# Two-layer decode kernel: stationary operands of up to 32 columns, gate and up as rows, and a new written-out order

## The chip, the cores and the metric

The kernel runs on one core of a Trainium2 chip, in one launch. The metric is device time in microseconds (us), the median over executions; lower is better. The profile and its trace are of one execution on that core. Engines are named as in the profile: PE (matrix products), DVE, ACT and POOL (vector work), SP (which issues the transfers); SPq is SP's queue.

## The reference, cut to what matters

Two layers with the same weights and the same K and V caches are run one after the other on 4 tokens (B = 4, one position each, D = 448):

```python
x = x + _A_ref(_layernorm(x), k_cache, v_cache, wq, wo)     # 16 query heads, 8 kv heads of 256
x = x + _B_ref(_layernorm(x), w_gate, w_up, w_down)         # (silu(x @ w_gate) * (x @ w_up)) @ w_down, F = 1792
x = x + _A_ref(_layernorm(x), k_cache, v_cache, wq, wo)
x = x + _B_ref(_layernorm(x), w_gate, w_up, w_down)
```

Attention looks only at the last 2048 of 8192 cached positions: `q = x @ wq`, scores `q k / 16`, softmax, times v, then `@ wo`. So each token has, for each of 8 kv heads, 1 MB of K and 1 MB of V; both layers read the same ones. All data are bf16.

## The kernel before, in words

**Storage and loads.** K and V come in halves of 512 KB: two K halves and two V halves for each token and kv head. A pool of 31 slots holds such halves; 7 further slots of the same size first hold `wq`. Of a token's 8 heads the K and V of 6 stay in their slots from layer 0 to layer 1 (`KEEP_K`, `KEEP_V`), so 160 half loads are made and not 256. All transfers go through SP's one queue, in the order of `SEQ_SP` (L121), and `SLOTS` (L130) gives the slot of each. `schedule` (L235) makes a load wait for the last PE operation that reads what its slot held before (`rel`): scores for a K half, a PV operation for a V half. SP works in order, so a load that waits holds back every load behind it.

**The unit of work: a group of two kv heads** (`group`, L929), written `t l k`, so `010+011` is token 0, layer 1, heads 0 and 1. DVE transposes each K half in place (L948). POOL spreads the query over the columns of `qe` (L987). PE makes the scores S (L982): 32 products of 128 rows by 8 columns with 256 moving columns, four quadrants of the array side by side. DVE takes the maximum, PE spreads it (L1000, L1003), DVE negates it, ACT makes the exponentials (L1013), PE turns them (L1026), ACT copies them to `pT` (L1035), PE and DVE sum them, PE multiplies with V in four operations PV00, PV01, PV10, PV11 (L1057; 32 products in all, each operation for one V half). ACT and DVE pick the wanted rows (L1072, L1074), PE turns ("flip", L1080), DVE scales into a buffer `oT` (L1090). The out-projection of one kv head is either four products with `oT` as stationary operand ("oprow", L1110) or 16 products with `wo` as stationary operand ("opcol", L1102). There are two buffers `oT`; each kv head of a step takes the next in turn, and out-projections come at the end of the step.

**A boundary.** When the last group of a token's layer is done, the rows gathered in bank A are turned ("rowT", L857 to L871), added to the residual (L877), normed (L579 on), sent through the feed-forward part (`ffn`, L767) and normed again; the query projection (`qproj`, L643; 32 products of 512 moving columns, L671) gives the query of layer 1 by two turns (L687) and a spread ("qspread", L701), and a cast to `qc` (L706). Only then can the scores of that token's layer 1 run, and so free the slots of the six heads that were kept. Gate and up (L785) each take 56 products with a 128x128 block of weights as stationary operand and 32 moving columns; tanh is made by ACT (L805), and down (L826) takes 56 products. With `late` (before: token 3 only, and the last layer) gate and up start from the raw residual, and a product `wm` corrects the mean afterwards; `QLATE` does the same for the query projection.

**The order.** `PLAN` lists steps of groups. What each engine does, and in which order, is written out by number in `SEQ_PE`, `SEQ_DVE`, `SEQ_ACT`, `SEQ_POOL` and `SEQ_SP` (L61 to L129); the durations in the code serve only to place the waits. A `w` in `SEQ_PE` is a filler (L1212 on, rows L1214): a product of 512 moving columns with a zero operand, accumulated into bank A, which keeps PE busy while it would wait. `HELD` (L136) says which operations on bank A stand behind which filler.

**Sequence of the tokens.** Token 0's layer 0, token 1's first heads, then the boundary of token 0; its layer 1 together with token 1's layer 0, and so on. While a token passes its boundary, PE works on one group of the next token, and SP loads ahead as far as slots are free. `wd`, the down weights, is the last weight to be loaded.

## Time and profile before

| | |
|---|---|
| median of 3 executions | 284.23 us (284.0 to 289.03) |
| the profiled execution: span | 283.0 us, some 1.2 us less than the median |
| mean granted PE clock | 0.895 |
| moved on SP's queue | 96.06 MB, busy for 88.0% of the span |
| PE busy | 210.4 us (74%) |
| DVE busy | 168.6 us (60%), of it 98.0 us in 80 transposes of K halves |
| ACT, POOL busy | 50.9 us, 77.2 us |
| fillers on PE (L1214) | 147, 51.0 us |
| scores (L982), PV (L1057) on PE | 40.8 us and 42.2 us, 1040 and 1024 products |

How to read it: the span runs from the first to the last instruction of one execution. Busy times of engines overlap. A busy PE is not a PE at its peak, since products are pipelined and their ends are modelled; four products that run side by side in the four quadrants count once. The granted clock is 1.00 at full speed and about half of that in cold stretches. In a window row come its bounds, its length, the busy time of each engine with the number of its instructions, the granted clock, the share of time that the 16 DMA engines were busy, and GB/s. In a row of an engine's timeline come start and length in us, engine, line, operation, output and inputs, shape and count; in square brackets stands the idle time before it and what ended it. Rows of waits give total, times and the longest. "xN" counts instructions.

### The profile page before, as it was taken

Reading aid. Unit: us, or ns where it says so; the run is one execution under the profiler, and the core shown is the slowest. Engines: PE = TensorE matmul, PEld = TensorE weight load, DVE = VectorE, ACT = ScalarE, POOL = GpSimd, SP = SyncE. Lnnn points to the kernel's source line nnn. Section 1 sums busy time; section 2 is a strip of 40 time slices with the busy share of each in tenths; the row PEclk is TensorE's granted clock in tenths of the full one; section 3 lists DMA queues with packets and bytes.
Section 4 is the critical chain, followed back from the end, with each engine's and each line's share of the span. In section 5 each row is a group of like instructions: output and inputs, shape, how many; then the busy total and the mean of one; then the engine's idle time right before and its main releaser. Section 6 shows DMA issues by size and latency. Waiting matters only on the chain.

```text
span 283.0 us, 9526 instructions
## 1 busy us (share of the span) xinstructions
PE 210.4 (74%) x4204; PEld 120.8 (43%) x4204; DVE 168.6 (60%) x511; ACT 50.9 (18%) x123; POOL 77.2 (27%) x202
## 2 busy tenths in 40 slices
PE   0757557586778886789887876798685787888986
PEld 0322124233644543347453432375453346554672
DVE  8745374158226795573755858656756378548831
ACT  0030002011102412112121212112130221034311
POOL 1352103001303432013253241123341221341650
PEclk9997757779789999799997979999795999999995
DMA  6999999999999999968799999948799997899300
GB/s 258 424 414 401 413 410 402 407 401 406 377 390 408 400 408 406 409 278 307 290 324 403 411 406 408 397 170 295 254 316 412 415 405 266 286 341 415 125 2 3
DMA packets 27752, 96.67 MB, mean 342 GB/s; under 512 B 2747, under 2 KB 6847, under 8 KB 26431
## 3 DMA queue, kind: packets, MB, share of 16 engines
q1 hardware_dynamic: 27703, 96.06, 88.0%
q8 instruction: 33, 0.54, 0.8%
q14 instruction: 8, 0.07, 0.1%
q10 hardware_dynamic: 8, 0.00, 0.0%
HBM read 96.05 MB, written 0.00 MB: 339 GB/s over the span
## 4 chain that ended last, share of the span: by engine, by line
DMA 30%; PE 27%; SPq 23%; DVE 12%; issue 3%; ACT 3%; POOL 0%
DMA half<-in_A_k_cache_dram 13%; DMA half<-in_A_v_cache_dram 11%; SPq L555 10%; DVE half L948 8%; SPq L958 8%; DMA wd_sb<-in_B_w_down_dram 6%; PE A L1214 5%; PE Y L1057 5%; PE S L982 4%; PE Z L785 3%; SPq L944 3%; SPq L942 3%; PE Z L826 2%; PE A L1110 2%; DVE oh L1074 1%
## 5 line engine op out<-in xcount | busy, mean ns | idle before, releaser
L948 DVE STREAM_TRANSPOSE half<-half 128x1024 uint32<-128x1024 uint32 x80 | 98.0, 1233 | 16.3 <-DMA half<-in_A_k_cache_dram 15.9
L1214 PE MATMUL A<-identb,small 128*128 128x512 bf16 x147 | 51.0, 452 | 7.4 <-DVE A L478 5.5
L1070 POOL TENSOR_TENSOR small<-small 128x4 f32<-128x4 f32 x32 | 32.4, 1015 | 68.0 <-DVE small L1048 61.7
L982 PE MATMUL S<-half,qe 128*8 128x256 bf16 (+1 forms) x1040 | 40.8, 305 | 12.0 <-DVE half L948 11.1
L1057 PE MATMUL Y<-half,pT 128*8 128x256 bf16 x1024 | 42.2, 296 | 7.3 <-DMA half<-in_A_v_cache_dram 3.9
L982 PEld LDWEIGHTS S<-half,qe 128*8 128x8 bf16 x1040 | 25.4, 92 | 26.1 <-DVE half L948 15.5
L987 POOL TENSOR_TENSOR qe<-qc,tiny 128x64 bf16<-128x64 bf16 x64 | 17.2, 292 | 60.1 <-PE S L982 46.4
L1013 ACT ACTIVATE praw<-S,small 104x256 bf16<-104x256 f32 x32 | 15.1, 473 | 81.7 <-DVE small L1009 81.2
L1057 PEld LDWEIGHTS Y<-half,pT 128*8 128x8 bf16 x1024 | 22.2, 90 | 17.8 <-DMA half<-in_A_v_cache_dram 5.3
L995 DVE TENSOR_REDUCE tiny<-S 104x1 bf16<-104x256 f32 x32 | 13.3, 418 | 19.0 <-PE S L982 19.0
L1072 ACT ACTIVATE oh<-Y 128x256 bf16<-128x256 f32 x32 | 12.3, 383 | 66.3 <-PE Y L1057 61.9
L1214 PEld LDWEIGHTS A<-identb,small 128*128 128x128 bf16 x147 | 13.0, 109 | 20.4 <-issue 7.4
L1074 DVE SCALAR_TENSOR_TENSOR oh<-oh,small,Y 128x256 bf16<-128x256 bf16 x32 | 15.0, 468 | 11.0 <-ACT oh L1072 10.4
L1110 PE MATMUL A<-wo_sb,oT 128*4 128x448 bf16 x220 | 17.2, 380 | 0.8 <-DVE oT L1090 0.6
L1080 PE MATMUL Y<-tiny,oh 128*128 128x4 bf16 x64 | 6.6, 172 | 15.1 <-DVE oh L1074 15.0
L1048 DVE TENSOR_REDUCE small<-Y 128x4 f32<-128x64 f32 x32 | 7.0, 218 | 13.8 <-PE Y L1043 12.1
L1026 PE MATMUL Y<-selt,praw 104*64 104x48 bf16 x256 | 10.1, 197 | 5.9 <-ACT praw L1013 5.5
L1080 PEld LDWEIGHTS Y<-tiny,oh 128*128 128x128 bf16 x64 | 4.2, 103 | 22.5 <-DVE oh L1074 19.6
L1035 ACT ACTIVATE pT<-Y 128x192 bf16<-128x192 f32 x32 | 10.5, 329 | 15.6 <-PE Y L1026 15.3
L1026 PEld LDWEIGHTS Y<-selt,praw 104*64 104x64 bf16 x256 | 6.7, 113 | 12.6 <-ACT praw L1013 9.9
L671 PE MATMUL Z<-half,xn 128*5 128x512 bf16 x160 | 10.2, 379 | 2.2 <-DVE st L606 0.8
L612 POOL TENSOR_SCALAR st<-st 128x1 f32<-128x1 f32 x16 | 4.4, 274 | 26.4 <-DVE st L606 26.4
(125 smaller groups left out, 219.7 us busy)
## 6 DMA issues: line engine op xcount, KB each, us to landing
half<-in_A_v_cache_dram SPq DMA_DIRECT2D x80, 512.0 KB, 12.1
half<-in_A_k_cache_dram SPq DMA_DIRECT2D x66, 512.0 KB, 10.3
half<-in_A_k_cache_dram SPq DMA_DIRECT2D x7, 1024.0 KB, 17.2
wo_sb<-in_A_wo_dram SPq DMA_DIRECT2D x8, 448.0 KB, 16.8
half<-in_A_wq_dram SPq DMA_DIRECT2D x3, 1024.0 KB, 9.0
wd_sb<-in_B_w_down_dram SPq DMA_DIRECT2D x1, 1568.0 KB, 17.1
wg_sb<-in_B_w_gate_dram SPq DMA_DIRECT2D x1, 1344.0 KB, 17.3
wu_sb<-in_B_w_up_dram SPq DMA_DIRECT2D x1, 1344.0 KB, 16.6
```

The source lines that it names most:

```text
L555: g.dma(rank, nbytes, lambda e: e.dma_start(dst, src), f"w{nw[0]}", w=key if isinstance(key, tuple) else (key,), run=run)
L948: return e.transpose(a, a)
L958: g.dma(pp + VLAG, 1 << 19, lambda e, cell=cell, hv=hv, vsrc=vsrc: e.dma_start(unit(cell), vsrc[hv]), None, w=(f"v{t}_{kvh}_{hv}",), run=4 ...
L982: last = e.matmul(Sb[s_][qd:qd + 8, c0:c0 + rhs.free_size()], lhsT=qe[q_][:, P, ce, :, :].rearrange("p a n -> p (a n)"), rhs=rhs, start=(c ...
L987: g.op(POOL, 0.25, pos - SLEAD - 1, lambda e, P=P, t=t, kvh=kvh: e.tensor_tensor(qe[q_][:, P, :, :, :], qc[t][:, kvh, :, :].unsqueeze(2).b ...
L1013: return e.activation(praw[0:R, 0:128 * n].rearrange("p (g r l) -> p g r l", g=2 * n, l=2), Sb[s_][0:R, 0:128 * n].rearrange("p (l g r) -> ...
L1026: last = e.matmul(Yb[p_][64 * h:64 * h + 64, c0:c0 + (48 if n == 2 else 32)], lhsT=praw[0:R, 64 * gg:64 * gg + 64], rhs=w, start=(gg == 0) ...
L1057: last = e.matmul(Yb[p_][32 * gg:32 * gg + M, 256:512], lhsT=pT[pt][:, gg, 2 * a + hv, 4 * P:4 * P + M] if n == 2 else p1[:, gg % 2, 2 * a ...
L1070: g.op(POOL, 0.69, pos, lambda e: e.tensor_tensor(ri[p_][:, 0:2 * n], rs[p_][:, 0:2 * n], expo[:, 1:1 + 2 * n], op=ALU.pow), r=(f"rs{p_}", ...
L1074: g.op(DVE, 0.43, pos, lambda e: e.scalar_tensor_tensor(out=oh[:, :], in0=oh[:, :], scalar=lomask[:, 0:1], in1=Yb[p_][:, 256:512], op0=ALU ...
L1110: last = e.matmul(Ab[32 * k:32 * k + B, 0:D], lhsT=oT[oi][:, k % 2, k // 2, :], rhs=wo_sb[:, 4 * kvh + k, :], start=False, stop=False, ski ...
L1214: return e.matmul(Ab[:, 0:512], lhsT=zero[:, 0:1].broadcast_to([128, 128]), rhs=identb[:, :].unsqueeze(1).broadcast_to([128, 4, 128]), sta ...
```

## The change

**Columns.** The stationary operands of scores, PV and query projection are read as up to 32 neighbouring columns of their buffer, and no longer as 8 (scores, PV) or 5 (query); the row out-projection reads up to 16, before 4. The further columns give further output rows within the same 32-row quadrant of the bank, which nobody reads. For this the buffers become flat (`qef`, `pTf`, `oTf`, `xnx`).

```diff
+COLS = 32
...
-lhsT = xn[:, cc, :]
...
-last = e.matmul(zb[32 * j:32 * j + B + 1, 0:512], lhsT=lhsT, rhs=wq_sb[:, c:c + 512],
+last = e.matmul(zb[32 * j:32 * j + x_cols(cc, j).shape[1], 0:512], lhsT=x_cols(cc, j), rhs=wq_sb[:, c:c + 512],
...
-last = e.matmul(Yb[p_][32 * gg:32 * gg + M, 256:512],
-                lhsT=pT[pt][:, gg, 2 * a + hv, 4 * P:4 * P + M] if n == 2 else
...
+c0 = 48 * gg + 12 * (2 * a + hv) + 4 * P
+c1 = min(c0 + COLS, 192)
+last = e.matmul(Yb[p_][32 * gg:32 * gg + c1 - c0, 256:512], lhsT=pTf[pt][:, c0:c1],
```

**Gate and up as rows.** The 112 products with weights as stationary operand become 32 products with x as stationary operand and 448 moving columns of weights, in four quadrants. Then come a copy of the gate's bank by ACT, a turn by PE, a copy of up's bank (one half by ACT, one by DVE), a second turn; the products `wm` of the late mean stand behind the turns. The down weights are laid out to match, and come in 6 transfers, before 1.

```diff
-for fc in range(NFC):
-    if cc < 3:
-        lhsT, x = w[:, cc * FF + fc * 128:cc * FF + fc * 128 + 128], xn[:, cc, sl]
...
+for j in range(4):
+    c = cc * FF + 448 * j if cc < 3 else 3 * FF + 448 * (j % 2)
+    last = e.matmul(zb[32 * j:32 * j + x_cols(cc, j).shape[1], 0:448], lhsT=x_cols(cc, j), rhs=w[:, c:c + 448],
+                    start=(cc == 0), stop=(cc == 3), skip_group_check=True)
...
+g.op(SCA, 0.54, rank, lambda e: e.activation(wideb[:, 0:448], Zb[:, 0:448], ACT.Copy), r=("z",), w=("wa",), bank=("Z",))
+g.op(PE, 0.16, rank, lambda e: turn(e, 0), r=("wa", "identb"), w=("z",), bank=("Z",))
+g.op(SCA, 0.31, rank, lambda e: e.activation(wideb[:, 512:736], Z2[:, 0:224], ACT.Copy), r=("z2",), w=("wb",), bank=("Z2",))
+vec(rank, lambda e: e.tensor_copy(wideb[:, 736:960], Z2[:, 224:448]), ("z2",), ("wb2",), 0.31, ("Z2",))
+g.op(PE, 0.16, rank, lambda e: turn(e, 1), r=("wb", "wb2", "identb"), w=("z2",), bank=("Z2",))
```

**Late means and the direct query.** `late` in the feed-forward part now holds for tokens 1, 2 and 3, and `QLATE` likewise; before it was token 3 alone. For tokens 0, 1 and 2 the `qe` of the first group of layer 1 is written by DVE straight from the bank of qspread, without the cast to `qc` and without POOL. With one token the query's scale is applied by the DVE operation behind the turns, so that the copies of the query's banks no longer wait for the scale.

```diff
-LATE = ((3, 0),)
-QLATE = (3,)
+LATE = ((1, 0), (2, 0), (3, 0))
+QLATE = (1, 2, 3)
+PRE = (0, 1, 2)
```

**Steps.** Steps of four kv heads become two steps of two. With four heads in a step and two buffers `oT`, the third and fourth head were written over the first and second before their out-projections; now each head has its buffer until it is projected. Code for groups of one head and for a feed-forward part over several tokens goes, and with it 7 set-up operations of DVE.

```diff
-    "000+001", "002+003 004+005", "006+007", "100+101", "012+013", "014+015", "016+017", "102+103", "104+105",
+    "000+001", "002+003", "004+005", "006+007", "100+101", "012+013", "014+015", "016+017", "102+103", "104+105",
...
-    "212+213 214+215", "216+217 302+303", "306+305", "304+307", "110+111", "210+211 316+313", "314+315",
+    "212+213", "214+215", "216+217", "302+303", "306+305", "304+307", "110+111", "210+211", "316+313", "314+315",
```

**The order.** All lists of the order are new: `SEQ_PE` (109 fillers, before 147), `SEQ_DVE`, `SEQ_ACT`, `SEQ_POOL`, `SEQ_SP` (177 entries, before 172; still 160 half loads, 14 of them as 7 pairs), `SLOTS` and `HELD`. What matters of it, with the place of a load given by the bytes that SP has issued up to it:

- At the start K comes ahead of V; `wq` comes at 11 to 14 MB and not among the first 5, and the last weight ends at 33.1 MB, before at 31.0.
- Before each boundary all K halves of the token come ahead of its V halves. The last V of token 1 stands at 48.9 MB (before 46.2), that of token 2 at 68.8 (before 67.2), that of token 3 at 85.0 (before 84.0).
- Scores 200+201 and 300+301, the group of the next token that runs inside a boundary, stand ahead of the boundary (before: behind opcol). Scores 010+011 (token 0, layer 1) stand directly behind opcol of token 1's boundary (before: behind the query projection), and PV 010+011 among the query's products. Scores 110+111 stand ahead of opcol of token 3's boundary.
- Behind boundary 0 loads run up to 36.8 MB until one waits for scores 012+013; in boundary 1 up to 51.5 MB until one waits for scores 010+011; in boundary 2 up to 74.6 MB, the last four of them freed by PV 300+301, until one waits for scores 212+213; in boundary 3 up to 87.1 MB until one waits for scores 110+111.

288 lines of the change are left out of this document (124 added, 164 removed), and 127 rows, old and new, of tables (SEQ_ACT, SEQ_DVE, SEQ_PE, SEQ_POOL).

## The prediction

> **What bounds the kernel now.** I read the page's head and queue table first, then busy time by windows, then SP's waits, SP's own timeline and PE's timeline around the four points where a token leaves its first layer.
>
> ```profile
> span 283.0 us, 9526 instructions
> PE 210.4 (74%) x4204; PEld 120.8 (43%) x4204; DVE 168.6 (60%) x511; ACT 50.9 (18%) x123; POOL 77.2 (27%) x202
> q1 hardware_dynamic: 27703, 96.06, 88.0%
> ```
>
> No engine is full, but one queue moves 96.06 MB and is busy 88% of the span. The windows (length; busy us and instructions of PE, PEld, DVE, ACT, POOL; granted PE clock; DMA share; GB/s) show where it is not:
>
> ```profile
> 0.00:84.00 84.00, 53.03 (x726) 25.47 (x727) 43.32 (x158) 8.81 (x19) 16.75 (x50) 0.82 1.00 392
> 84.00:124.00 40.00, 30.41 (x616) 16.11 (x615) 27.18 (x59) 9.31 (x22) 12.00 (x30) 0.96 1.03 406
> 124.00:150.00 26.00, 21.71 (x540) 14.48 (x538) 14.84 (x47) 4.69 (x11) 8.76 (x25) 1.00 0.78 288
> 150.00:184.00 34.00, 25.69 (x446) 13.23 (x446) 23.55 (x57) 6.95 (x18) 8.37 (x19) 0.90 1.02 407
> 184.00:214.00 30.00, 23.69 (x576) 15.90 (x574) 19.36 (x54) 5.91 (x14) 9.42 (x27) 0.94 0.78 267
> 214.00:238.00 24.00, 17.64 (x384) 10.37 (x385) 15.62 (x40) 4.22 (x11) 5.44 (x12) 0.87 0.95 380
> 238.00:254.00 16.00, 13.84 (x363) 9.88 (x359) 8.07 (x31) 3.53 (x8) 6.20 (x15) 1.00 0.91 306
> 254.00:266.00 12.00, 10.60 (x262) 6.47 (x261) 10.65 (x36) 4.32 (x11) 4.36 (x11) 1.00 0.85 342
> 266.00:283.00 17.00, 13.76 (x313) 8.89 (x310) 5.96 (x35) 3.14 (x9) 5.89 (x15) 0.77 0.01 3
> ```
>
> 406 GB/s is the full pace (1.29 us for a half head of 0.524 MB). A window loses its length times (1 - GB/s / 406): 7.6 us in 124-150, 10.3 us in 184-214, 1.5 in 214-238, 3.9 in 238-254, 1.9 in 254-266. These are the boundaries of tokens 1, 2 and 3: their loads stand behind scores that need the token's own second-layer query.
>
> ```profile
> SPq L958 <- PE Z L599: 30.8, 2, 15.9
> SPq L958 <- PE Z L586: 29.5, 3, 14.6
> ```
> ```profile
> 108.47 18.81 SPq L958 DMA_DIRECT2D half<-in_A_v_cache_dram  x4
> ...
> 168.04 19.53 SPq L958 DMA_DIRECT2D half<-in_A_v_cache_dram  x4
> ...
> 222.25 0.77 SPq L942 DMA_DIRECT2D half<-in_A_k_cache_dram  x1
> 237.36 1.05 SPq L958 DMA_DIRECT2D half<-in_A_v_cache_dram  x2
> ```
> ```profile
> DMA to landing us min/median/max: 3.2/12.1/18.9
> ```
>
> SP stands in front of a V load for some 15 us at each boundary (the waits are booked to the norm's products, which PE does next to the scores that really free the slot), and a load issued into a dry queue needs at least 3.2 us to land. So the time is made of the stream's pace, of how far the slots reach at each boundary, and of what follows the last boundary. PE's rows for these points:
>
> ```profile
> 81.39 1.56 PE L826 MATMUL Z<-wide,wd_sb 128*128 128x32 bf16 x56 [1.41 <-DMA wd_sb<-in_B_w_down_dram]
> ...
> 88.35 0.24 PE L701 MATMUL Z<-wide,fold 128*32 128x128 bf16 x4
> ...
> 89.89 1.12 PE L982 MATMUL S<-half,qe 128*8 128x256 bf16 x32
> ...
> 121.32 1.05 PE L1057 MATMUL Y<-half,pT 128*8 128x256 bf16 x32
> ...
> 124.58 0.95 PE L1102 MATMUL A<-oT,wo_sb 128*128 128x1 bf16 x32
> ...
> 127.66 1.22 PE L785 MATMUL Z<-xn,wg_sb 128*128 128x32 bf16 x42
> ...
> 131.33 1.56 PE L826 MATMUL Z<-wide,wd_sb 128*128 128x32 bf16 x56
> ...
> 185.03 0.94 PE L1102 MATMUL A<-oT,wo_sb 128*128 128x1 bf16 x32
> ...
> 200.03 3.55 PE L982 MATMUL S<-half,qe 128*8 128x256 bf16 x64 [0.70 <-POOL qe L987]
> ...
> 235.24 0.54 PE L1102 MATMUL A<-oT,wo_sb 128*128 128x1 bf16 x16
> ...
> 250.01 0.24 PE L701 MATMUL Z<-wide,fold 128*32 128x128 bf16 x4 [0.28 <-DVE wide L694]
> ```
>
> L1102 (opcol) opens a boundary, L701 (qspread) gives the next query. The last qspread ends at 250.25; the 32.75 us behind it are five groups and the last FFN, latency and PE, and hardly any transfer.
>
> **Part 1, columns.** S, PV and q load 1040 + 1024 + 160 = 2224 stationary operands of 8 or 5 columns, now up to 32; the count of products is unchanged.
>
> ```profile
> L982 PEld LDWEIGHTS S<-half,qe 128*8 128x8 bf16 x1040 | 25.4, 92 | 26.1 <-DVE half L948 15.5 <-POOL qe L987 2.5 <-DVE xr L871 0.4
> ...
> L1214 PEld LDWEIGHTS A<-identb,small 128*128 128x128 bf16 x147 | 13.0, 109 | 20.4 <-issue 7.4 <-DVE A L478 5.5 <-ACT wide L857 3.6
> ...
> L701 PEld LDWEIGHTS Z<-wide,fold 128*32 128x32 bf16 x20 | 0.5, 92 | 2.2 <-DVE wide L694 2.0
> ```
>
> A load of 32 columns takes 92 ns like one of 8; one of 128 takes 109. Bounds: nothing, or 17 ns on each of 556 rounds of four (9.5 us if none hides, some half of it on the path); below nothing only if wider operands bought clock, and rival 2 shows no room for that. I take nothing, by the row of equal width. The Trainium skill ("TensorE: Matmul & The Clock Gate", section "LDWEIGHTS (loading the stationary operand)") gives a load as its columns divided by 1.2 ns, so 27 ns instead of 7; by it I would estimate 556 rounds by 20 ns, 11 us, and a sum of up to 290. The two equal rows do not agree with it, though they may hold a fixed cost that hides the difference. The row out-projection (220 products) goes the same way.
>
> **Part 2, gate and up as rows.** 112 products of 32 columns become 32 of 448 in four quadrants, plus copies and turns.
>
> ```profile
> L671 PE MATMUL Z<-half,xn 128*5 128x512 bf16 x160 | 10.2, 379 | 2.2 <-DVE st L606 0.8 <-DMA half<-in_A_wq_dram 0.8 <-DVE xn L589 0.5
> L785 PE MATMUL Z<-xn,wg_sb 128*128 128x32 bf16 x280 | 8.4, 179 | 0.3 <-DVE xn L849 0.3
> ```
> ```profile
> L857 ACT ACTIVATE wide<-A 128x448 bf16<-128x448 f32 x8 | 4.3, 543 | 12.5 <-PE A L1110 12.5
> ```
>
> q's products have the new shape: 10.2 us / 160 = 64 ns each for 512 columns, 56 for 448, so 32 of them 1.8 us. Gate alone was 8.4 / 5 = 1.7 us, both 3.3. The gate's copy (0.54, L857's size) lies beside up's products; up's copy is split over ACT and DVE (about 0.4), then a turn (0.25). Gate's start to down was 131.33 - 127.66 = 3.7 us; now 1.8 + 0.4 + 0.25 + 0.2 for the two products of the late mean + 0.2 for tanh's end = about 3.1. Gain 0.6 us a boundary; bounds -0.5 (a turn waits for ACT or DVE) to 1.4.
>
> **Part 3, late means, query direct, split steps.** LATE and QLATE for tokens 1 and 2 let gate/up and q start from raw values. Bounds 0 to 3.5 us a boundary: token 3 has both already, and its boundary is as long, 250.01 - 235.24 = 14.8, as token 2's 200.03 - 185.03 = 15.0, since transposes stand in DVE's order there. I take 0.5. The direct write of qe by DVE drops a cast and a POOL product; of the 89.89 - 88.59 = 1.3 us from qspread to scores it saves about 0.5. Split steps and 7 fewer set-up operations cost nothing that the stream does not cover. 38 of 147 fillers go; PE has room without them (rival 2).
>
> **Part 4, the order, which carries the sum.** Counted along the new SP list, bytes are the same.
>
> ```profile
> 64.22 17.12 DMA wd_sb<-in_B_w_down_dram
> ```
>
> Boundary 0: the last weight lands at 81.34; it moves from 31.0 to 33.1 MB, so 86.5. Scores 012+013 ended 91.0 - 81.4 = 9.6 us after down began; less 0.5 that is 95.7, and the loads behind them land at 98.9. The slots reach 36.8 MB, to 95.6: 3.3 us lost that were not lost before (406 GB/s in 84-124).
> Boundary 1: L is the landing of the last V (48.9 MB). From there to opcol 2.6 us (124.58 - 122.37 = 2.2 behind PV, and some 0.4 of PV's 1.05), opcol 0.95, then scores 010+011 directly, 1.12: L + 4.7, plus 3.2. Free slots reach 51.5 MB, 6.4 us: 1.5 lost; up to 3.5 with the transposes of K 011 in the way (they land 2.6 us after L). I take 2.4 instead of 7.6: gain 5.2.
> Boundary 2: opcol at L + 2.6; to scores 212+213 15.0 - 1.1 (scores 300+301, now ahead) - 0.6 - 0.5 - 0.5 = 12.3; they end at L + 16.0, their loads land at L + 19.2. The slots, with those that PV 300+301 frees, reach 5.8 MB, 14.3 us: 4.9, with a cold clock as at 200.03 5.6. I take 5.3 instead of 10.3: gain 5.0.
> Boundary 3: the last V of token 3 moves from 84.0 to 85.0 MB. By the windows' sums 85.0 MB had landed at 233.0 and 84.0 at 230.5, so qspread ended 19.8 us after that V. The 0.6 of part 2 goes against scores 110+111, now ahead of opcol: 19.8 again.
>
> **Sum.** 233.0 + 3.3 - 5.2 - 5.0 = 226.1; + 19.8 = 245.9 for the last qspread (before 250.25). Behind it 32.75 - 0.4 (rows in the last FFN, where the norm's chain ends last) = 32.35: span 278.2. The execution shown has span 283.0, the median is 284.23, 1.2 above it: 279.5 us.
>
> **Rivals.** 1, larger gain: LATE, QLATE and the direct query yield their full 3.5 us at boundaries 2 and 3, less what the slots then limit, about 5 us in all: 274.5. For it: three latency steps go; against: token 3's 14.8 us.
> 2, the other side, the clock. Fillers:
>
> ```profile
> 120.23 0.60 PE L1214 MATMUL A<-identb,small 128*128 128x512 bf16 x2
> ...
> 280.27 1.03 PE L1214 MATMUL A<-identb,small 128*128 128x512 bf16 x2
> ```
> ```profile
> 87.04:111.00 23.96, 1.15 (x3) 0.29 (x3) 1.00 1.02 405
> ```
>
> The same two products take 1.03 us in a cold stretch and 0.60 in a warm one; 64 scores at 200.03 took 3.55 where two rows of 32 make about 2.1: 1.4 us for one cold stretch. Seven such on the path (two at each of three boundaries, one in the tail) are 9.8 us: 289.3; four already cost the gain. Against it: from 87 to 111 three fillers were enough for a clock of 1.00.
> 3, new waits inside boundaries: V 201.1 is freed by scores 010+011 (L + 4.7), lands at L + 7.9 and is wanted ahead of up's turn at about L + 8.8; transposes of late K stand before the boundary's own DVE work. One miss of 3.2 + 1.23 us: 284.
> 4, wide loads pace the streams: the 9.5 us of part 1, nearly all on the path: 288.5; by half, 284.
> 5, widening does nothing at all: that is what I forecast for part 1, with the order alone giving the gain.
>
> **Chances.** Forecast 0.48 (own range 276 to 283), larger gain 0.18, new waits 0.20, clock 0.09, wide loads 0.05. About 2% (278.5, 289.9) can be told from no change: faster 0.38 (0.18 and two fifths of the forecast), slower 0.09 (two thirds of the clock case, a third of the wide loads, a little of the waits), same 0.53. Range 272.5 to 287.5: the larger gain and the waits with their halves to each side, leaving out most of the clock case.
>
> **What would show it.** Right: about 3 us lost near 96 us, 2 to 3 in the boundary of token 1, 5 to 6 in that of token 2; the last qspread near 246; loads of 32 columns near 92 ns; gate to down near 3.1 us. Wrong: granted clock under 0.9 between 124 and 254; PE or DVE idle for a V or K half inside a boundary; rows of 32 scores above 1.2 us at full clock; qspread before 243.

## The result, and the profile after

| | before | changed |
|---|---|---|
| median, on the same chip | 284.12 us (4 executions) | 292.39 us (4 executions) |
| ratio | | 1.0304 [1.0229, 1.038] |
| span of the profiled execution | 283.0 us | 289.2 us |
| mean granted PE clock | 0.895 | 0.91 |

The forecast was 279.5 us; the kernel became 3% slower. Medians stand over all executions, among them some that were disturbed (longer by some per cent), which ratios leave out (so a ratio need not be the quotient of two medians); below, the profiled executions of e9, e11 and e12 are disturbed ones, of e12's four executions only one, of 289.37 us, is not, and half of e13's ten are.

The page of the changed kernel, head, engines and queue:

```profile
span 289.2 us, 8772 instructions
...
PE 204.7 (71%) x3820; PEld 112.4 (39%) x3820; DVE 170.6 (59%) x519; ACT 54.1 (19%) x133; POOL 75.8 (26%) x195
...
q1 hardware_dynamic: 27783, 96.06, 87.4%
```

The same 96.06 MB, fewer instructions, less work on PE, in this execution a slightly higher clock (the executions of 292.18 and 292.61 us had 0.87 and 0.876), and still 6.2 us more. So I looked at when the bytes came. Busy time by windows, with the bounds used before the prediction:

```profile
0.00:84.00 84.00, 38.31 (x541) 18.41 (x541) 44.03 (x144) 8.56 (x19) 16.90 (x50) 0.91 1.00 383
84.00:124.00 40.00, 30.66 (x523) 16.31 (x526) 25.64 (x60) 6.61 (x17) 7.95 (x22) 0.71 0.87 319
124.00:150.00 26.00, 21.81 (x407) 11.38 (x398) 10.72 (x39) 6.08 (x17) 7.19 (x14) 0.93 0.84 317
150.00:184.00 34.00, 28.80 (x611) 16.24 (x606) 27.13 (x70) 7.45 (x18) 11.15 (x32) 1.00 1.02 394
184.00:214.00 30.00, 25.52 (x523) 14.74 (x520) 19.70 (x61) 6.98 (x17) 8.95 (x23) 1.00 0.89 344
214.00:238.00 24.00, 18.84 (x375) 10.21 (x363) 13.48 (x34) 4.81 (x13) 7.10 (x14) 0.93 1.02 393
238.00:254.00 16.00, 12.88 (x254) 7.37 (x250) 9.41 (x35) 3.17 (x8) 3.27 (x9) 0.89 0.84 301
254.00:266.00 12.00, 9.96 (x250) 6.85 (x246) 9.63 (x30) 3.79 (x9) 4.21 (x13) 1.00 0.93 332
266.00:289.20 23.20, 17.89 (x392) 10.94 (x384) 10.89 (x50) 6.63 (x18) 9.10 (x21) 0.90 0.16 64
```

The window 84-124, at full pace before (406 GB/s), now has 319: 87 GB/s over 40 us are 3.5 MB, 8.6 us at the full pace. The boundaries of tokens 1 and 2 did improve: 317 for 288, 344 for 267. The first 84 us have 383 for 392, 0.76 MB or 1.9 us.

Windows shift against each other once a kernel is late. The surest comparison is the time at which equal bytes had landed (the completion events of the transfers, added up along SP's list):

| MB landed | before, us | changed, us | later by | added in this stretch | forecast for it |
|---|---|---|---|---|---|
| 33.1 (last weight of the changed kernel) | 86.45 | 89.33 | 2.9 | +2.9 | 0 |
| 39.9 (past boundary 0) | 103.24 | 114.78 | 11.5 | +8.7 | +3.3 |
| 48.9 (last V of token 1) | 126.04 | 138.05 | 12.0 | +0.5 | 0 |
| 58.3 (past boundary 1) | 156.87 | 165.13 | 8.3 | -3.8 | -5.2 |
| 68.8 (last V of token 2) | 182.43 | 192.06 | 9.6 | +1.4 | 0 |
| 85.0 (last V of token 3) | 233.03 | 237.99 | 5.0 | -4.7 | -5.0 |
| last qspread | 250.25 | 257.0 | 6.8 | +1.8 | +2.6 |
| end | 283.0 | 289.2 | 6.2 | -0.6 | -0.4 |

Of the 11.9 us by which 85.0 MB came later than forecast, 8.2 arose ahead of 39.9 MB. Here is that place in the changed kernel, PE's timeline and then windows, whose last two numbers are the busy share of the DMA engines and GB/s:

```profile
89.92 1.65 PE L813 MATMUL Z<-wide,wd_sb 128*128 128x32 bf16 x56 [0.42 <-issue]
...
98.62 0.24 PE L728 MATMUL Z<-wide,fold 128*32 128x128 bf16 x4 [0.21 <-DVE wide L716]
...
99.32 2.05 PE L969 MATMUL S<-half,qe 128*32 128x256 bf16 x64 [0.46 <-DVE qe L976]
```
```profile
98.70:104.70 6.00, 4.72 (x127) 3.44 (x131) 5.29 (x12) 1.61 (x4) 2.08 (x8) 1.00 0.47 151
104.70:112.20 7.50, 4.89 (x114) 2.90 (x112) 4.50 (x9) 1.10 (x4) 2.65 (x5) 1.00 0.94 299
112.20:138.00 25.80, 18.67 (x309) 9.38 (x309) 14.68 (x34) 4.38 (x12) 5.37 (x11) 0.74 1.03 411
```

Down began at 89.92 (before 81.39), qspread at 98.62 (before 88.35), and the load behind scores 012+013 was issued at 100.50, not at 95.7. The slots had reached 36.8 MB, landed at 98.69; the next half landed at 104.92. The second row is the surprise: from 104.7 to 112.2 the DMA engines are busy for 94% of the time, but move 299 GB/s and not 411. The halves behind the dry queue landed at 104.92, 107.59, 110.81 and 112.22, and only then every 1.28 us. So boundary 0 cost 5.0 us of dry queue (6.2 us from 98.69 to 104.92, less the 1.28 of a half at full pace) and 3.4 us of slow refill (7.3 us for three halves, which take 3.8 at full pace).

### The profile page after: what moved, and what is told of

Same layout as the page of the kernel before. It is cut to its first block, busy times and chain, and to the rows that moved or that the text cites. A ratio compares the mean times of both kernels' runs of the same rounds, so it can differ in the third digit from the quotient of the medians.

```text
span 289.2 us, 8772 instructions
## 1 busy us (share of the span) xinstructions
PE 204.7 (71%) x3820; PEld 112.4 (39%) x3820; DVE 170.6 (59%) x519; ACT 54.1 (19%) x133; POOL 75.8 (26%) x195
## 3 DMA queue, kind: packets, MB, share of 16 engines
q1 hardware_dynamic: 27783, 96.06, 87.4%
## 4 chain that ended last, share of the span: by engine, by line
DMA 30%; PE 27%; SPq 18%; DVE 17%; issue 3%; ACT 2%; POOL 2%; POOLq 0%; ACTq 0%
DMA half<-in_A_v_cache_dram 19%; DVE half L934 10%; SPq L944 7%; DMA wu_sb<-in_B_w_up_dram 6%; SPq L565 6%; PE Y L1048 5%; DMA half<-in_A_k_cache_dram 5%; PE Z L689 4%; PE A L1185 3%; PE S L969 3%; SPq L930 2%; PE A L1100 2%; PE Z L813 2%; SPq L928 2%; PE Z L757 2%
## 5 line engine op out<-in xcount | busy, mean ns | idle before, releaser
L1048 PE MATMUL Y<-half,pT 128*32 128x256 bf16 (+4 forms) x1024 | 47.9, 297 | 12.1 <-DMA half<-in_A_v_cache_dram 9.6
L1059 POOL TENSOR_TENSOR small<-small 128x4 f32<-128x4 f32 x32 | 32.4, 1016 | 56.4 <-DVE small L1038 36.8
L1185 PE MATMUL A<-identb,small 128*128 128x512 bf16 x109 | 42.6, 431 | 1.0 <-issue 0.4
L969 PE MATMUL S<-half,qe 128*32 128x256 bf16 (+4 forms) x1040 | 36.9, 285 | 6.8 <-DVE half L934 3.6
L1048 PEld LDWEIGHTS Y<-half,pT 128*32 128x32 bf16 (+4 forms) x1024 | 21.5, 99 | 26.9 <-DMA half<-in_A_v_cache_dram 14.7
L969 PEld LDWEIGHTS S<-half,qe 128*32 128x32 bf16 (+3 forms) x1040 | 26.4, 96 | 12.8 <-DVE half L934 4.3
L1100 PE MATMUL A<-wo_sb,oT 128*16 128x448 bf16 (+2 forms) x220 | 18.6, 375 | 2.8 <-DVE oT L1079 1.9
L689 PE MATMUL Z<-half,xn 128*32 128x512 bf16 (+2 forms) x160 | 14.8, 505 | 3.2 <-DMA half<-in_A_wq_dram 3.2
L1185 PEld LDWEIGHTS A<-identb,small 128*128 128x128 bf16 x109 | 10.0, 105 | 15.4 <-issue 14.0
L614 PE MATMUL Z<-st,small 128*128 128x2 f32 x32 | 7.3, 297 | 11.9 <-DVE xn L604 7.4
L1079 DVE TENSOR_TENSOR oT<-Y,small 128x4 bf16<-128x4 f32 x64 | 8.2, 156 | 10.3 <-PE Y L1069 9.8
```

Of the source, the lines that this page charges most:

```text
L689: last = e.matmul(zb[32 * j:32 * j + x_cols(cc, j).shape[1], 0:512], lhsT=x_cols(cc, j), rhs=wq_sb[:, c:c + 512], start=(cc == 0), stop=(c ...
L969: last = e.matmul(Sb[s_][qd:qd + q1 - q0, c0:c0 + rhs.free_size()], lhsT=qef[q_][:, q0:q1], rhs=rhs, start=(ce == 0 and i == 0), stop=(ce ...
L1048: last = e.matmul(Yb[p_][32 * gg:32 * gg + c1 - c0, 256:512], lhsT=pTf[pt][:, c0:c1], rhs=unit(vss[P][hv])[:, 1024 * a + 256 * gg:1024 * a ...
L1059: g.op(POOL, 0.69, pos, lambda e: e.tensor_tensor(ri[p_][:, 0:2 * n], rs[p_][:, 0:2 * n], expo[:, 1:1 + 2 * n], op=ALU.pow), r=(f"rs{p_}", ...
L1100: last = e.matmul(Ab[32 * k:32 * k + 16 - c0, 0:D], lhsT=oTf[oi][:, c0:], rhs=wo_sb[:, 4 * kvh + k, :], start=False, stop=False, skip_grou ...
L1185: return e.matmul(Ab[:, 0:512], lhsT=zero[:, 0:1].broadcast_to([128, 128]), rhs=identb[:, :].unsqueeze(1).broadcast_to([128, 4, 128]), sta ...
```

## The experiments

Theories. O: the new order loses it, by weights that end later and by boundary 0, which empties the queue. C: the wide columns cost it. Clock: the cold stretch in boundary 0 (0.71 in 84-124) does. Later came two more: rows and their six transfers, and VectorE's transposes. Edits of the written lists are shown with labels: "K 106.1" is the second K half of token 1, layer 0, head 6, "T" its transpose on DVE, "12+" a group. "Stretch" is the time from opcol of token 0 to opcol of token 1, 53.2 us before and 64.8 in the changed kernel.

| run | edit | median us | ratio to before | stretch | 39.9 MB | 85.0 MB |
|---|---|---|---|---|---|---|
| e1 | 8 columns | 290.73 | 1.02 [1.0125, 1.0275] | 59.5 | 111.5 | 233.1 |
| e2 | loads behind the weights | 294.7 | 1.0318 [1.0242, 1.0394] | 64.3 | 113.5 | 238.4 |
| e3 | 15 more fillers | 294.82 | 1.033 [1.0254, 1.0406] | 61.6 | 114.0 | 239.8 |
| e4 | before, weights later | 288.56 | 1.0141 [1.0062, 1.022] | 58.1 | 110.4 | 236.9 |
| e5 | e2 with other places | 291.0 | 1.0229 [1.0157, 1.0301] | 66.1 | 112.0 | 234.9 |
| e6 | old order, new code | 298.28 | 1.0408 [1.0327, 1.0489] | 57.0 | 108.0 | 237.4 |
| e7 | e6 with 8 columns | 299.15 | 1.0516 [1.0456, 1.0576] | 54.9 | 107.4 | 237.0 |
| e8 | e5, two T behind the query | 293.3 | 1.0318 [1.0246, 1.039] | 64.9 | 113.9 | 238.4 |
| e9 | gate and up as columns | 287.89 | 1.0171 [1.011, 1.0232] | 58.6 | 109.7 | 236.9 |
| e10 | e9 with the moves of e8 | 290.01 | 1.0277 [1.0202, 1.0352] | 64.1 | 105.6 | 239.0 |
| e11 | e9, softmax ahead of T | 297.21 | 1.0351 [1.0215, 1.0486] | 66.2 | 109.4 | 245.5 |
| e12 | e10, softmax ahead of T | 294.82 | too few for one | 68.3 | 107.0 | 242.9 |
| e13 | down weights in one transfer | 289.3 | 1.0117 [1.0025, 1.021] | 61.9 | 113.1 | 235.6 |
| e14 | old order, columns alone | 284.95 | 1.005 [1.0005, 1.0096] | 54.0 | 105.7 | 233.9 |
| e15 | e10 with 8 T cut | 286.38 | 1.0101 [1.003, 1.0171] | 56.7 | 103.9 | 230.8 |
| e16 | changed, 8 T cut | 291.42 | 1.0144 [1.0032, 1.0256] | 62.5 | 115.5 | 237.7 |
| e17 | e10, scores 200+201 later | 287.78 | 1.0066 [1.0016, 1.0116] | 62.9 | 107.3 | 234.4 |

Stretch and landings of each run are of its one profiled execution.

**Columns: e1, e7, e14.**

```diff
-COLS = 32
+COLS = 8
```

> The changed kernel with stationary operands of 8 columns again in scores, PV, query, gate and up (one constant). Theory O (the new order costs the time: weights end 8 us later, boundary 0 dries the queue): no difference, 290 to 294 us. Rival C (wide loads pace PE's streams, worth 9.5 us by the bound of the prediction): 283 to 288 us. The other way, if 32 columns count as more activity for the clock: 295 or more, with a lower granted clock.

290.73, which lies in theory O's range, but the ratio is 1% under that of the changed kernel, with intervals that overlap: a price of 1% for the columns is neither shown nor excluded, and 85.0 MB landed 4.9 us earlier in its one profiled execution. The pair e6 and e7 looks for it in another order. Both are the new code with the old order, the old steps (four heads, which overwrite two) and 147 fillers:

```diff
-LATE = ((1, 0), (2, 0), (3, 0))
-QLATE = (1, 2, 3)
-PRE = (0, 1, 2)
+LATE = ((3, 0),)
+QLATE = (3,)
+PRE = ()
...
-PLAN, SEQ_PE, SEQ_DVE, SEQ_ACT, SEQ_POOL, SEQ_SP, SLOTS of the changed kernel
+those of the kernel before, the new operations put in behind gate and up
```

> The new code in the order of before: operands of 32 columns and gate and up as rows, with the down weights in 6 transfers, but the old steps, the old order of every engine and of SP, the old slots and 147 fillers, late means for token 3 only and no direct query (the old steps of four heads overwrite as before). Theory O (parts 1 and 2 cost little, part 4 costs the 8 us): 283 to 286 us. Rival C or R (wide loads, or the rows' copies and turns, cost the time): 288 us or more.

> As the run in the old order, with operands of 8 columns: gate and up as rows alone. Against that run: by the prediction (32-column loads cost nothing) the same within 1 us; by the wide-load bound 3 to 9 us faster. Against before: by the 0.6 us a boundary of the prediction 282 to 284.5; if the chain of copies and turns is longer than the products it replaces, 285 to 287.

298.28 with 32 columns, 299.15 with 8: no price of the columns in this pair. That the old order does not carry the rows is the other finding: there the new operations had no place of their own, gate to down took 4.4, 3.8 and 6.8 us for tokens 1, 2 and 3 (before 3.7, 3.2 and 4.6), and the part behind the last qspread 38.5 us (before 32.75). e14 is the old order with the columns and without the rows:

```diff
-16 products of 448 columns for gate, 16 for up, copies and turns
+the 112 products with 32 moving columns, one transfer of the down weights
```

> The kernel before with its own order, steps, fillers, gate and up as columns and one transfer of the down weights, with stationary operands of up to 32 columns and the query's scale behind the turns as the only parts of the change (the four-head steps overwrite two heads as in the kernel before). Part 1 of the prediction (columns cost nothing): 283 to 286, ratio 0.995 to 1.005. Wide loads cost (rival 4): 288 or more. With the earlier run of the old order with rows (298.3) this gives the price of the rows where the order was not written for them: about 13 us if this run is near 284.

284.95, ratio 1.005: the columns alone (with the query's scale behind the turns) cost at most 1%. Here are load rows of e1, with 8 columns, and then of the changed kernel:

```profile
L969 PEld LDWEIGHTS S<-half,qe 128*8 128x8 bf16 x1040 | 23.8, 87 | 15.0 <-DVE half L934 4.7 <-POOL qe L983 2.5 <-ACT praw L1010 1.3
L1048 PEld LDWEIGHTS Y<-half,pT 128*8 128x8 bf16 x1024 | 20.2, 89 | 25.7 <-DMA half<-in_A_v_cache_dram 11.0 <-issue 5.3 <-DVE small L1038 3.8
```
```profile
L969 PEld LDWEIGHTS S<-half,qe 128*32 128x32 bf16 x842 | 25.9, 97 | 12.5 <-DVE half L934 4.3 <-POOL qe L983 2.5 <-ACT praw L1010 1.3
L1048 PEld LDWEIGHTS Y<-half,pT 128*32 128x32 bf16 x896 | 21.5, 99 | 26.9 <-DMA half<-in_A_v_cache_dram 14.7 <-issue 4.9 <-DVE small L1038 3.4
```

A load of 32 columns takes 97 and 99 ns where one of 8 takes 87 and 89. So it is 10 ns longer, but most of that does not reach the time: in e14, where the same rows have 100 and 105 ns (92 and 90 before), the kernel is at most 1% slower. Theory C is out as the cause of the 3%.

**Clock: e3.** Fifteen more fillers between opcol and the query of boundary 0.

```diff
+w w w w w w w w w w w w w w w
```

> The changed kernel with 15 more fillers in boundary 0, where the granted clock was 0.5 from 80 to 97 us. Rival K (the boundary is slow because the clock is cold): clock 1.0 there, boundary 0 shorter by 2 to 4 us, 288 to 290.5 us. Theory O alone (the weights arrive at 89.3 whatever the clock is): down at the same time, query projection 1.7 us shorter, 290 to 292; if the fillers stand in the way, 293.

The window of e3 shows that the clock was mended (0.86, before the edit 0.71) and the stream barely (335 GB/s for 319, and 406 before the change):

```profile
84.00:124.00 40.00, 30.01 (x549) 16.18 (x547) 26.52 (x60) 7.37 (x18) 8.77 (x22) 0.86 0.92 335
```

294.82: no gain in the time. The boundary itself did become shorter, as the first half of the query projection shows, in the changed kernel and in e3:

```profile
93.42 1.90 PE L689 MATMUL Z<-half,xn 128*32 128x512 bf16 x16
```
```profile
93.11 1.05 PE L690 MATMUL Z<-half,xn 128*32 128x512 bf16 x16
```

From down's start to the load behind scores 012+013 it is 9.2 us in e3 (89.66 to 98.90) and 10.6 in the changed kernel. The cold clock of boundary 0 thus cost 1.4 us there, a small part of what was lost. At 68.8 MB e3 is 2.9 us ahead of the changed kernel, and it loses that again in boundary 2 (85.0 MB 1.8 us later), which the edit does not touch.

**Weights earlier: e2, e5, e8, and weights later in the kernel before: e4.**

```diff
 SEQ_SP, e2
-K 103.0 K 107.0 V 100.0 V 100.1 ahead of the feed-forward weights
+K 103.0 K 107.0 V 100.0 V 100.1 behind them, T 103.0 and T 107.0 later as well; PV00 and PV01 of 100+101 behind down
 SEQ_SP, e5
+V 100.1 V 100.0 ahead of V 101.0, K 103.0 K 107.0 ahead of K 104.0; all four PV of 100+101 behind down
 SEQ_DVE, e8 (on top of e5)
+T 104.0 T 201.0 behind the cast of the query
 SEQ_SP, e4 (kernel before)
+V 100.0 V 101.1 K 102.0 ahead of the feed-forward weights
```

> The changed kernel with four half loads (K 103.0, K 107.0, V 100.0, V 100.1; 2.1 MB) moved from ahead of the feed-forward weights to right behind them, and PV00, PV01 of 100+101 behind down. Theory O: the last weight lands 5 us earlier (84 instead of 89.3), scores 012+013 release slots 5 us earlier while the queue runs dry at the same byte, so 284 to 288 us. Rival C or K (clock): at most 1 us, since the stream itself is unchanged: 291 to 293.

> The kernel before with three half loads (V 100.0, V 101.1, K 102.0; 1.57 MB) moved ahead of the feed-forward weights, nothing else. Theory O: the last weight 3.9 us later; slots reach the same byte, so about 1 us of slack at boundary 0 is used up and then some 3 us plus a slow refill are lost: 287 to 290 us. Rival (a shift of the weights is absorbed by later stalls, since the boundaries behind wait anyway): 284 to 285.

> The changed kernel with the same 2.1 MB (K 103.0, K 107.0, V 100.0, V 100.1) behind the feed-forward weights, but V 100 directly behind them, K 103.0 and K 107.0 behind V 101 and K 201.0, and the four PV of 100+101 spread between down and the query projection, so that none waits for its V. Theory O: last weight at 83.5, down at 85.5, scores 012+013 at about 95 instead of 99.3, little or no dry queue (39.9 MB landed at 108 to 110 instead of 114.8), 285 to 288 us. If it stays at 291 to 294, the late weights are not what the boundary costs.

> As the second run with the weights 2.1 MB earlier, and the transposes of K 104.0 and K 201.0 moved in DVE's order from ahead of the query's spread to behind it (in that run the spread waited 2.8 us for the transpose of K 104.0, whose load lands at 94.7 us). Theory O (the boundary of token 0 and the dry queue behind it cost the time): scores 012+013 at about 94, no dry queue, 39.9 MB landed at 105 to 107, 286 to 289 us. If it stays above 290, what the first boundary loses is lost later anyway.

e4 did as theory O says: 1.57 MB ahead of the weights made the kernel before 4 us slower, 39.9 MB landing 7.1 us later. The reverse in the new order failed three times: last weight at 83.5, 84.4 and 84.7 instead of 89.3, and 294.7, 291.0, 293.3 us. In e2 PE then waited for the V of group 100+101, in e5 the query waited 2.8 us for DVE, which did two transposes ahead of it; e8 took those away and won nothing. But in none of the three did boundary 0 end much sooner: the load behind scores 012+013 was issued at 98.6, 98.2 and 99.1, against 100.5 in the changed kernel, and 39.9 MB landed at 112 to 114. So theory O in its simple form, that earlier weights alone bring the time back, fell; what a boundary 0 that does end sooner is worth, these runs do not show (e10 does).

**Rows and their six transfers: e9, e13.** e9 has gate and up as columns in the new order, with one transfer of the down weights; e13 has the rows and one transfer. In e13 the rows of the down weights then lie in another order than the products of down take them, so its output is not that of the kernel; the operations of the engines and the bytes are the same.

```diff
-for j in range(4):
-    load(rank_d, 344064, wd_sb[:, 3 * j:3 * j + 3, :], ...
-for h in range(2):
-    load(rank_d, 114688, wd_sb[64 * h:64 * h + 64, 12:14, :], ...
+load(rank_d, 1605632, wd_sb[:, :, :], B_w_down.rearrange("(c p) n -> p c n", p=128), ..., 430)
```

> The changed kernel and its new order with gate and up as columns again (112 products, no copies and turns, one transfer for the down weights); operands of 32 columns stay elsewhere. Theory R (rows cost: 1.9 us for the six transfers and 1 to 1.5 us in each boundary for copies and turns): 286 to 289 us. The prediction's part 2 (rows gain 0.6 us a boundary): 293 to 295 us. Theory O alone: 291 to 293.

> The changed kernel with the down weights in one transfer of 1.6 MB, as before, in place of six (the bytes are the same, but the rows of w_down then lie in another order than the products take them, so down multiplies with the wrong rows; nothing else differs). If the six transfers make the weights late by the 1.9 us that the landings at equal bytes suggest and the lateness goes through to the end: the last weight lands near 87.4 in place of 89.3 and the time is 289 to 291. If the order of token 1's work takes the gain back, as in the variants with moved weights: last weight near 87.4, the time 291.5 to 293.5. If six smaller transfers cost nothing: last weight at 89 still.

e13: 289.3 us and a ratio of 1.0117 [1.0025, 1.021], which does not reach that of the changed kernel. The first 84 us of e13:

```profile
0.00:84.00 84.00, 41.34 (x558) 19.61 (x558) 44.51 (x147) 9.03 (x20) 16.90 (x50) 0.88 1.00 390
```

390 GB/s for 383: 0.6 MB, 1.4 us, and the same 33.1 MB at 87.89 instead of 89.33. Six transfers of the same bytes make the weights late, and this lateness goes through to the end (85.0 MB at 235.6 for 238.0, span 286.7 for 289.2 us). The old order agrees: last weight at 83.8 in e6 (rows, six transfers) and 81.5 in e14 (columns, one). e9 (287.89) and e13 overlap, so beyond the transfers no price of the rows themselves is shown. From 33.1 to 39.9 MB e13 still loses 8.4 us.

**What follows boundary 0: e10.** The moves of e8 in e9.

> Both edits together: gate and up as columns with one transfer of the down weights, and the 2.1 MB and the two transposes behind the weights and the spread. If O and R are both true and add: 281 to 285 us, at or below before; if they take the same stall, 285 to 288.

Here boundary 0 was healed: 39.9 MB at 105.6, two us behind the kernel before and nine ahead of the changed one. But token 1's last V landed at 127.8 and its opcol came only at 136.2, and the time was 290.01. Of the 9 us, 5.3 were left at 58.3 MB (159.8 for 165.1) and none at 85.0 (239.0 for 238.0). The second loss lies in boundary 2, where the granted clock was 0.50 for 17 us; whether the clock is its cause was not tried:

```profile
193.00:210.00 17.00, 14.68 (x239) 7.79 (x239) 8.44 (x26) 1.85 (x4) 3.45 (x13) 0.50 0.37 143
```

Where the first loss arose, show DVE's timeline and PE's (start, length, and in brackets the idle time before):

```profile
93.25 4.61 DVE L916 STREAM_TRANSPOSE half<-half 128x1024 uint32<-128x1024 uint32 x4
...
105.24 4.61 DVE L916 STREAM_TRANSPOSE half<-half 128x1024 uint32<-128x1024 uint32 x4
```
```profile
98.23 0.22 PE L980 MATMUL S<-small,identb 104*104 104x32 bf16 x1 [2.65 <-DVE tiny L975]
...
110.38 0.20 PE L1051 MATMUL Y<-tiny,oh 128*128 128x4 bf16 x2 [2.06 <-DVE oh L1045]
...
116.69 1.12 PE L951 MATMUL S<-half,qe 128*32 128x256 bf16 x32 [2.00 <-DVE half L916]
```

PE waits for maxima and head steps that DVE does behind four transposes, and then for a transpose. Two theories: the order on DVE (D), or its amount of work (A).

**DVE's order: e11, e12.** Softmax steps ahead of the transposes, in e9 and in e10.

```diff
 SEQ_DVE between the cast of the query and the sums of 104+105
-T 106.1 T 107.1 T 106.0 | negm 102+ | oh2 012+ | T 105.0 | oT | T 200.0 | rs 016+ | T 105.1 | oT | T 010.1 | oh2 014+
+T 106.1 | negm 102+ | T 107.1 | oh2 012+ | T 106.0 | oT oT | rs 016+ | oh2 014+ | T 105.0 T 105.1 T 104.1
...
-T 104.1 T 200.1 | max 106+ | T 010.0 | max 104+ ...
+max 106+ ... oh2 016+ | oT oT | T 200.0 T 200.1 T 201.1 | ... | T 010.1 T 010.0
```

> The changed kernel with gate and up as columns (287.9 us before this edit) and one more edit: in VectorE's written order between the query spread of token 0 and the last column of token 1's output, the row maxima, their negation and the head steps stand ahead of the transposes of keys that stood before them (16 transposes of 1.23 us; the same work in another order). Theory D (behind boundary 0 the order on VectorE holds TensorE: it waited 1.9 us for a transpose, 1.5 us for the head steps and 0.9 us for sums there): the stretch from the output column of token 0 to that of token 1 falls from 58.6 us to about 56, the time to 284.5 to 287. Theory S (loads set that stretch, the order on VectorE does not matter): 57.5 to 60 us for the stretch, the time 287 to 289. If the transposes put back free their buffers later, the loads behind them come later and the time is above 289.

> The same reordering on VectorE in the variant whose boundary 0 was healed by moved loads (290.0 us before this edit; there TensorE waited 2.65 us for row maxima behind four transposes, 2.06 us for a head step behind four more, 2.00 us for a transpose, and token 1's output column came 8.4 us after its last value load landed at 127.8). Theory D: the stretch from output column 0 to output column 1 falls from 64.0 us to 58 to 60, the column comes 4 to 5 us after the last value load, and the time is 284 to 287, since the loads of boundary 1 are then released earlier. Theory S, or a chain of softmax steps on the other engines: the stretch stays at 62 us or more and the time within 1.5 us of 290.

Neither became faster: e11 took 297.21 us, with an interval that just touches that of e9, and e12 294.82, at best 289.37, where e10 has 290.01. The stretch grew in both, to 66.2 and 68.3 us, where theory D had it fall. The waits of e12's profiled execution between 92 and 140 fit that: PE waited for transposes, at longest ahead of scores 200+201, which stand ahead of products with V on PE and whose transposes now came last.

```profile
PE S L951 <- DVE half L916: 9.8, 3, 4.9
```

Theory D found no support: a wait for the softmax steps became a longer one for a transpose.

**DVE's amount: e15, e16.** Eight transposes (keys 200, 201, 010, 011) cut to a quarter, in e10 and in the changed kernel. Three quarters of each of these key halves are left untransposed, so their scores are wrong.

```diff
+TRIM = ((2, 0, 0), (2, 0, 1), (0, 1, 0), (0, 1, 1))
...
 a = unit(cell).bitcast(UINT32).rearrange("p (k s) -> p k s", k=32)
+a = a[:, 0:8, :] if trim else a
```

> The variant with healed boundary 0 (290.0 us, 64.0 us from output column 0 to output column 1), and eight of the 16 to 20 transposes of that stretch (keys 200, 201, 010 and 011) cut to a quarter of their columns: the other three quarters are not transposed, so these scores are wrong. VectorE has 0.9 us less for each, about 6 us less up to scores 200+201. Theory A (the amount of work on VectorE, 24.8 us busy of 28.3, sets that stretch, whatever its order): the stretch falls to 58 to 60 and the time to 285 to 287. Theory P (PE's written order, in which each V product stands behind score groups of later heads, sets it, with the loads of V): the stretch stays above 62 and the time at 289 to 291.

> The same cut of eight transposes in the changed kernel as it is (292.4 us), where token 1's output column came 3.6 us after its last value load landed at 138.05. Theory: the loads set that stretch here, so it falls by less than 2 us from 64.9 and the time is 290.5 to 293. If VectorE's work sets it here as well: 60 us or less for the stretch and a time of 288 or less.

The stretch after boundary 0 in e10, and the same in e15:

```profile
92.00:121.00 29.00, 18.71 (x371) 10.74 (x368) 25.14 (x44) 4.68 (x12) 7.06 (x17) 0.83 0.96 379
121.00:137.00 16.00, 13.69 (x248) 7.42 (x245) 6.93 (x22) 3.24 (x10) 4.11 (x8) 0.88 0.73 290
```
```profile
92.00:121.00 29.00, 22.41 (x463) 13.91 (x455) 21.73 (x47) 6.39 (x17) 8.64 (x20) 0.88 1.02 403
121.00:137.00 16.00, 14.21 (x339) 9.25 (x335) 6.07 (x31) 3.01 (x9) 4.53 (x10) 1.00 0.92 347
```

In e10 DVE is busy 25.1 of 29 us; with less transposing the stretch falls from 64.1 to 56.7 us, more than the 6.4 us taken off DVE (eight transposes of 0.43 us for 1.23), and the stream stays at 403 GB/s. 85.0 MB had landed at 230.8, 2.2 us ahead of the kernel before. Theory A holds for e10. (The kernel is still 1% slower than the one before: its last qspread ended at 251.5, 20.7 us behind 85.0 MB, where it was 17.2 before.) In the changed kernel itself (e16) the same cut took the stretch from 64.8 to 62.5 and the time to 291.42: there the loads, late by boundary 0, set most of it. The two limits lie one behind the other, which is why healing the first alone gave nothing in e10.

**A whole kernel with less on DVE in that stretch: e17.**

```diff
 SEQ_PE
-flip 016+ | S 200+ | ... | spread 200+ | ... | PV01 104+ | ... | PV01 106+ | flip 104+
+flip 016+ | ... | PV01 104+ | S 200+ | ... | PV01 106+ | spread 200+ | flip 104+ | turn 200+
 SEQ_DVE
+T 200.0 T 200.1 T 201.0 T 201.1 T 010.1 T 010.0 behind the head steps of 016+ and 102+
```

> The variant with healed boundary 0 and gate and up as columns (290.0 us), with scores 200+201 and their softmax steps moved on TensorE from behind the flip of 016+017 to behind the second product with V of 104+105, and the transposes of keys 200, 201 and 010 moved on VectorE behind the head steps of 016+017 and of 102+103. All work is done. Theory A (VectorE's work ahead of scores 200+201 delays token 1): the stretch from output column 0 to output column 1 falls from 64.0 to 57 to 60 us, and the time to 285 to 288; keys 011 are then freed some 3 to 4 us later, which stays hidden as long as 51.5 MB has landed before the first scores of token 0's second heads end. Rival: the transposes are only moved to where they delay output column 1 itself (it stands behind them on VectorE), the stretch stays above 62 and the time within 1.5 us of 290. If keys 011 come too late and with them the whole of boundary 1: above 292.

```profile
92.00:121.00 29.00, 21.48 (x429) 12.85 (x428) 21.58 (x44) 5.29 (x14) 8.88 (x20) 0.82 0.96 375
121.00:137.00 16.00, 11.93 (x225) 6.42 (x217) 11.39 (x28) 2.62 (x7) 2.36 (x5) 0.89 0.77 295
```

The work left the first 29 us of DVE (21.6 for 25.1) and came back in the next 16 (11.4 for 6.9): the stretch stayed at 62.9, as the rival said, while the time, 287.78, is in theory A's range. The profiled executions differ mostly in boundary 2 (68.8 to 80.3 MB took 36.8 us, in e10 40.5, where a cold stretch of 17 us lay), so the gain over e10 is not shown to come from the move. It is the best complete variant of the new order, and not faster than the kernel before; none of the runs was.

## Why the prediction was wrong, point by point

**What bounds the kernel**: right. The stream with its boundaries set the time after as well, and the loss could be read from it.

**Part 1, columns at nothing**: right for the time within 1% (e6 and e7, e14). The reading under it, that a load of 32 columns takes as long as one of 8, was off by 10 ns (e1 and the changed kernel). The Trainium skill ("TensorE: Matmul & The Clock Gate", section "LDWEIGHTS (loading the stationary operand)") gives a load's ns as its columns divided by 1.2, so 27 for 32 columns. The trace does not agree for these loads: 97 and 99 ns.

**Part 2, a gain of 0.6 us a boundary**: not found. The terms listed for gate to down add up to 2.85 us and not to 3.1. The products cost what was forecast, the steps behind them more. Boundary 2, PE and then ACT:

```profile
195.37 0.75 PE L757 MATMUL Z<-wg_sb,xn 128*32 128x448 bf16 x12
...
197.48 0.36 PE L757 MATMUL Z<-wu_sb,xn 128*10 128x448 bf16 x4
...
198.45 0.40 PE L1048 MATMUL Y<-half,pT 128*32 128x256 bf16 x8
198.79 0.36 PE L769 MATMUL Z<-identb,wide 128*128 128x4 bf16 x5
...
199.53 1.56 PE L813 MATMUL Z<-wide,wd_sb 128*128 128x32 bf16 x56 [0.26 <-DVE wide L804]
```
```profile
197.89 0.36 ACT L782 ACTIVATE wide<-Z 128x224 bf16<-128x224 f32 x1 [0.57 <-PE Z L757]
```

Gate to down took 4.2 us (before 3.2): from the end of up's products at 197.84 to down at 199.53 lie 1.7 us, forecast 0.85 and some 0.1 for a product of the late mean, since copy, turn, mean product and the product with tanh's result follow one another, with a product with V between. For tokens 1 and 3 it was 5.4 and 5.2 us (before 3.7 and 4.6). Not all of that is the rows: with the late mean gate starts earlier, and other products stand between. In the old order, with the early mean for tokens 1 and 2 in both, rows took 4.4 and 3.8 us (e6) and columns 3.7 and 3.2 (e14), so there the sign was wrong. In the new order columns took 5.8 to 6.9 us for tokens 1 to 3 (e9 to e12, e15, e17) and rows 4.2 to 6.8 (changed kernel, e1 to e3, e5, e8, e13, e16), so there the rows are not shown to be the longer. And a part of the edit that has no term in the forecast, the six transfers of the down weights, cost 1.4 us at the last weight and 2.4 us at 85.0 MB (e13).

**Part 3**: the late means and the direct query shortened opcol to qspread together with the moved scores from 16.8, 14.0 and 15.0 us (tokens 1, 2 and 3, opcol's start to qspread's end) to 15.7, 11.6 and 14.4, so within the bounds of 0 to 3.5 us.

**Part 4, boundary 0 (3.3 us forecast, 8.7 measured, behind 2.9 at the start)**: the step that failed. Its terms: the last weight at 89.33 for 86.5, as the stream was slower in the first 84 us (six transfers account for 1.4, the rest is open); down 0.6 us behind it, where 0 was taken; from down to the freed slots 10.6 us, where 9.2 was taken (the cold clock, by e3, which has 9.2); the first load into the dry queue 4.4 us to its landing (100.50 to 104.92), where 3.2 was taken; and the refill behind it, taken at full pace at once, lost 3.4 us more. The 3.3 was itself too high by the forecast's own numbers: from 95.6 to 98.9 it counts the landing of a half, which takes 1.3 us at full pace too, so 2.0 us were to be lost. The same 1.3 us stand in the sums for boundaries 1 and 2, so without that slip the forecast would have been lower still.

**Part 4, boundaries 1 and 2**: right in mechanism. Boundary 2 gained 4.7 us (forecast 5.0), boundary 1 3.8 (5.2). That boundary 2 comes so near is partly luck: the forecast allowed for a cold clock there, which the profiled execution did not have (1.00 from 184 to 214), and counted the 1.3 us of a half as lost.

**Part 4, what was missing**: that all K of a token ahead of its V puts the transposes of token 1 and of the next groups into the time right behind boundary 0, on DVE, ahead of its softmax steps. I counted the order along SP's list alone. This is not a term of the changed kernel's own loss, where the loads came first, but it is a part of why healing the loads did not give the forecast (e10 and e15).

**The tail**: right; 85.0 MB to the last qspread 19.0 us (19.8), from there to the end 32.2 (32.35).

**The rivals**: on the slower side stood the clock (289.3) and the wide loads (288.5), both short of 292.4. The clock was not the reason, though it had a share: the profiled execution lost 6.2 us at a mean clock above that of before, and the one cold stretch that was mended was worth 1.4 us, the price that the forecast gave for one. New waits inside boundaries was nearest in kind, but at 284 far too small, and in the wrong boundary.

Open stays what makes the refill slow, whether the columns cost up to 1% in the new order (e1), what the other 1.5 us of the start beside the six transfers are, what the cold stretch in boundary 2 of e10 has to do with its time, and how the last 1 to 2% of e9 and e13 divide among order, steps and late means. No run mended boundary 0 in the changed kernel with its rows, so the cost of that boundary is read from landings and not from a run without it.

## What to carry to other kernels

When a list of loads is reordered, count every engine that works along that list, not the queue alone: transposes that follow the K loads moved with them. Price each layout change by its transfers too; splitting one transfer of 1.6 MB into six cost 2.4 us at 85.0 MB in a kernel that the stream bounds. And price a boundary up to the time at which the stream is back at its pace, since a cure for the first of two limits in a row shows nothing in the time.

## What the runs showed of the hardware

Behind a dry queue the stream does not return to its pace at once: busy share 0.94 and 299 GB/s for 7.5 us, with 411 after it. The kernel before has such a stretch too, behind its boundary 2: a load was issued at 187.24 and landed at 190.47, the next half at 193.04, and the two behind it every 1.2 to 1.3 us. It is the rule here: in the profiled executions of both kernels and all runs I count 36 places where the queue had run dry and four halves or more were then issued before the first had landed. The first landed 3.1 to 5.7 us after its issue, and the next three took 4.8 to 7.8 us (median 5.4), at none of them the 3.8 us of full pace; the changed kernel's boundary 0, with 7.3, is among the slowest. The cause was not tried. The granted clock was 0.50 from 84 to 89 us and 0.56 from 89 to 98 in the changed kernel, and mending that (e3) made the boundary 1.4 us shorter, without a gain in the time:

```profile
84.00:89.00 5.00, 4.82 (x28) 1.39 (x28) 0.82 (x4) 0.83 (x3) 0.00 (x0) 0.50 1.08 367
89.00:98.00 9.00, 8.43 (x131) 4.14 (x129) 4.29 (x16) 1.58 (x3) 1.29 (x5) 0.56 0.84 319
```
